# The last product of a two-layer token mixer in seven block products, under a new order of the whole program

## Chip, cores and metric

The program runs on one core of one Trainium2 chip. The metric is the device time of one execution in microseconds (us); the kernel before takes 1402.06 us, the median of three runs (1402.04 to 1402.17). Engines are named as the profile names them: PE (TensorE matmuls), PEld (its weight loads), DVE (VectorE), ACT (ScalarE), POOL (GpSimd), SP (the queue that issues the DMAs).

## The reference, cut

```python
# attention: q, k, v of 8 batches x 8 heads x 576 tokens x 64
out = A @ Z @ C @ v            # softmaxes against 32 landmarks; Z by 6 Newton steps
# first layer, x: 8 x 576 x 512
u  = x + real(fft2(x))
un = normalize(u)
x  = u + relu(un @ w_ch1) @ w_ch2                     # 512 -> 2048 -> 512
# second, gated layer
xk = mu_k * x + (1 - mu_k) * x_prev                   # x_prev: the token before
xr = mu_r * x + (1 - mu_r) * x_prev
k  = relu(xk @ w_k)                                   # 512 -> 1024
v  = k * k @ w_v                                      # 1024 -> 512
out = sigmoid(xr @ w_r) * v
```

## The kernel before

**Stages.** The 4608 tokens are nine blocks of 512 (`NB`, `BLK`). First come the eight batches of the attention (`phase1`, line 730) with the first layer of each block as soon as its tokens are there; batches below `HALF` (line 40) take their Fourier transforms with plain matrices and f32 products, the later ones fold the tokens into halves and use f16 pairs. Then comes the gated stage, one `Gated` object per block (line 1996 on).

**Numbers as pairs.** A value of f32 precision is a pair of f16 tiles, high and low half. A product is the three partial products of `PARTS`. A "split" makes the pair: ACT casts to the high half, DVE or POOL subtracts it for the low half.

**Seven block products.** Both operands are cut in 2 x 2 blocks of 256; sums of blocks are formed and seven products take the place of eight. The first-layer products from block 2 on, the product with `w_k` (`Gated.first`, line 2060) and the gate's with `w_r` (`Gated.gate`, line 2006) are made so. One such product is 12 matmuls of 256 columns. The product of the squared values with `w_v` (`Gated.second`, line 2114, and `last`) is a plain one: per block 8 rows f x 4 token groups j x 3 parts, 96 matmuls of 512 columns into four PSUM banks (`acc`); `store` (line 2143) multiplies each bank by `qi` and the sigmoid `sg` on DVE and issues the output DMA. `first` leaves the squared values as an f16 pair `k2`: per half g and quarter, ACT makes relu and square (`out`, line 2075) and the cast, DVE the low half.

**What sets the order.** Nothing is issued while the program is recorded. `Plan.record` notes every operation with its engine, cost and predecessors, and `Plan.issue` (line 469) simulates the engines with these costs: at each step the engine that is free first takes, of its ready operations, the one with the largest key, the longest way to the end (`tail`) plus a lead, by stage (`NOW` 1000, `SOON` 300, ...) and by part and batch (`LEADS`, line 155). The order so found is written out, one queue per engine. Matmuls marked `chain=True` (line 429) are each a predecessor of the next, so the main products keep the order in which the code records them. `HOP` 0.2 is added between engines; DVE operations that overlap a POOL operation are lengthened (lines 579 to 589). Where PE has a predicted gap, matmuls on zeros (`warm`, line 1423, tile `spare`) are put in.

**The gated stage's order.** `prep(i)` (line 1930) loads a block of the stored first-layer result (`yb`), mixes it with the token before (DVE, ACT) and splits seven sums each for `xk` and `xr`, the low halves on POOL; both operands alternate between two pools. `fillers` (line 2156) lays the steps of `first`, `gate` and the earlier block's `second` between one another.

**Rows of the profile.** Every ACT, DVE and POOL operation is issued in line 267, matmuls in 423, transposes in 440, DMAs in 408.

Of the kernel before, what the change touches and what calls it, by code (L numbers as in the profile page):

```python
# [24 lines left out]
DM = H * D  # L25
# [14 lines left out]
HALF = 2  # L40
# [100 lines left out]
class Op:  # L141
    def __init__(self, index, eng, run, cost, port=0, nbytes=0):
        self.index, self.eng, self.run, self.cost = index, eng, run, cost
        self.port, self.nbytes = port, nbytes
# [3 lines left out]
        self.parted = False  # L148

# [6 lines left out]
    ("back", 0): 808,  # L156
    ("back", 1): 3753,
    ("back", 2): 292,
    ("back", 3): 2,
    ("back", 4): 804,  # L160
    ("back", 5): 255,
    ("back", 6): 170,
    ("back", 7): 349,
    ("keys", 1): -347,
    ("keys", 2): 842,
    ("keys", 3): -200,
    ("keys", 4): -24,
    ("keys", 5): -20,
    ("keys", 6): 10,
    ("keys", 7): 107,  # L170
    ("land", 0): -297,
    ("land", 1): -653,
    ("land", 2): -89,
    ("land", 3): -333,
    ("land", 4): -544,
    ("land", 5): -74,
    ("land", 6): -180,
    ("land", 7): -185,
    ("norm", 0): 138,
    ("norm", 1): 3084,  # L180
    ("norm", 3): -30,
    ("norm", 4): 102,
    ("norm", 6): 511,
    ("norm", 7): -99,
    ("norm", 8): -30,
    ("own", 1): 500,
    ("own", 2): 23,
    ("own", 3): -84,
    ("own", 4): 146,
    ("own", 5): 150,  # L190
    ("own", 6): -6,
    ("own", 7): 404,
    ("pairs", 0): -315,
    ("prep", 1): 70,
    ("prep", 2): 140,
    ("queries", 1): 90,
    ("queries", 2): 148,
    ("queries", 3): 85,
    ("queries", 4): -18,
    ("queries", 5): 301,  # L200
    ("queries", 6): 622,
    ("queries", 7): 11,
    ("series", 1): 1044,
    ("series", 2): -102,
    ("series", 3): -103,
    ("series", 4): -41,
    ("series", 5): -137,
    ("series", 6): -95,
    ("sums", 0): 7,
    ("sums", 1): -85,  # L210
    ("sums", 2): 30,
    ("sums", 3): 448,
    ("w1", 1): -468,
    ("w1", 2): 34,
    ("w1", 3): 376,
    ("w2", 0): 5,
    ("w2", 1): -312,
    ("w2", 3): 246,
# [7 lines left out]
class Engine:  # L226
# [5 lines left out]
    def cost(self, op, outs, ins):  # L232
# [4 lines left out]
        if self.kind == "v":  # L237
            if op in ("tensor_scalar", "tensor_copy") and not psum:
                return (n / 2 + 150) / 960, 2
            if op == "reciprocal":  # L240
                return 0.25, 0
            return (n + 150) / 960, int(read > 1 and op != "tensor_reduce")
        if self.kind == "s":
            scalars = sum(wide(x) == 1 for x in ins) if n > 1 else 0
            more = 0.19 if len(outs) > 1 else 0.0
            more += 0.16 if outs[0].dtype == I8 else 0.05 if ins[0].dtype == I8 else 0.0
            return (0.17 if psum else 0.2) + n * 0.83e-3 + 0.093 * scalars + more, 0
        if op == "memset":
            return 0.1, 0
        return max(0.28, 0.15 + n * 2.28e-3), int(n > 8)  # L250

    def __getattr__(self, op):
        f = getattr(self.eng, op)

        def call(out, *args, **kw):
# [5 lines left out]
            cost, port = self.cost(op, outs, ins)  # L261
# [7 lines left out]
            return self.plan.record(self.kind, run, cost, outs, ins, port)  # L269
# [4 lines left out]
class Plan:  # L274
# [4 lines left out]
    HOP = 0.2  # L279
# [99 lines left out]
    def record(self, eng, run, cost, outs, ins, port=0, nbytes=0):  # L379
        op = self.node(eng, run, cost, port=port, nbytes=nbytes)  # L380
# [34 lines left out]
    def mm(self, out, lhsT, rhs, start, stop, chain=False, beside=1, **kw):  # L415
# [53 lines left out]
    def issue(self):  # L469
# [6 lines left out]
        for op in ops:  # L476
            for p in op.preds:
                p.succs.append(op)
        for op in reversed(ops):
# [12 lines left out]
        shared = both = dma = 0.0  # L492
        warming, parted = [], False

        def ready(op):
# [3 lines left out]
                    p.end + (self.HOP + op.slack if p.eng and p.eng != op.eng else 0.0)  # L499
# [15 lines left out]
        def done(op, end):  # L515
            op.end = end
            for t in holds.pop(op, ()):
                t.left -= 1
                if t.left == 0:
                    bank[t.bank] = max(o.end for o in t.ops) + self.HOP  # L520
# [30 lines left out]
        while any(avail.values()) or any(later.values()) or pending:  # L551
# [27 lines left out]
            free[e] = end = start + op.cost  # L579
            if e == "g" and op.port:  # L580
                shared = end
                if both > t:
                    free["v"] += 0.5 * min(both - t, op.cost)
            elif op.port and shared > t:
                over = shared - t
                end += min(0.5 * over, op.cost) if op.port == 1 else min(0.6 * over, 0.5)
                free[e] = end
            if e == "v" and op.port:
                both = end
# [140 lines left out]
def phase1(a, iss, psum, const, pool, ident, ublock, ones, early):  # L730
# [385 lines left out]
    def chain_c(b):  # L1116
# [56 lines left out]
        for g in range(2):  # L1173
            for c in range(5):
                kk = 128 if c < 4 else 64
                for hh in range(4):
# [5 lines left out]
                        c in (0, 2), c in (1, 4), tile_position=(0, 32 * hh),  # L1182
# [193 lines left out]
def build(nc, tc, a):  # L1376
# [5 lines left out]
    with stack, tc.manual_schedule():  # L1382
# [36 lines left out]
        iss.warm_from = g_.memset(zero, 0.0)  # L1419
        iss.lead = START  # L1420
# [16 lines left out]
        def rows_of(name, r, g):  # L1437
# [4 lines left out]
            "w_v0": [128, 2, 4, DM], "w_v1": [128, 2, 4, DM],  # L1442
# [39 lines left out]
        far_items = [  # L1482
# [820 lines left out]
```

## Time and profile before

| | us |
|---|---|
| median of three runs | 1402.06 |
| span of the profiled execution | 1401.8 |
| PE busy | 1389.2 |
| DVE busy | 1019.0 |
| ACT busy | 807.3 |
| POOL busy | 456.3 |
| matmuls on zeros | 23.6 |

A row of a timeline begins with its start and its length in us. Matmuls follow one another before the earlier one has ended, so the distance of two starts is what a matmul costs, and its length is more. A row of the chain has the start, the time up to the next link, engine, tile, line and count. A row of windows gives a stretch and its length, the busy time of PE, PEld, DVE, ACT and POOL with the count of instructions in brackets, the granted clock of PE, and the share and GB/s of the DMA engines. A row of a group gives the count, the busy time with the mean in ns of one, and the idle time before it.

### The profile page before, as it was taken

The page shows a single profiled execution, that of the slowest core. Times are in us where ns is not written, and L with a number is a line of the kernel's source. Part 1 is how long each engine was busy: PE and PEld are TensorE (multiplying, and loading weights), DVE is VectorE, ACT ScalarE, POOL GpSimd, SP SyncE. Part 2 cuts the span into 40 slices and gives each one's busy share as a digit, 9 for nine tenths or more (in the row PEclk, how much of TensorE's full clock was granted, in tenths as well). Part 3 has the DMA queues.
Part 4 walks back from the last instruction along what each step waited for, and adds up shares of the span by engine and source line. Part 5 has one row for each costly group of instructions (what it writes and reads, how often), then busy time and mean ns, then how long its engine had stood idle before and what let it go on. Part 6 is the DMA issues. An engine that isn't in the chain of part 4 may idle for free.

```text
span 1401.8 us, 26994 instructions
## 1 busy us (share of the span) xinstructions
PE 1389.2 (99%) x10648; PEld 906.1 (65%) x10648; DVE 1019.0 (73%) x2055; ACT 807.3 (58%) x1603; POOL 456.3 (33%) x546
## 2 busy tenths in 40 slices
PE   9999999999999999999999999999999999999998
PEld 5555454576676676676676666666767767776775
DVE  7897985886987876976966566837679788786332
ACT  4876543445545545545553445526787877786552
POOL 3013163532523422423332030603445552444000
PEclk9999999999999999999999999999999999999999
DMA  9795673655554554653556776423011011100001
GB/s 353 272 329 187 229 264 102 211 195 190 190 199 139 197 204 127 248 174 118 172 186 246 240 270 235 157 82 121 31 50 62 12 61 61 61 1 31 31 8 54
DMA packets 87071, 213.71 MB, mean 152 GB/s; under 512 B 7200, under 2 KB 28704, under 8 KB 80672
## 3 DMA queue, kind: packets, MB, share of 16 engines
q1 hardware_dynamic: 86944, 211.98, 43.4%
q8 instruction: 84, 1.38, 0.4%
q14 instruction: 43, 0.35, 0.1%
HBM read 168.71 MB, written 43.25 MB: 151 GB/s over the span
## 4 chain that ended last, share of the span: by engine, by line
PE 97%; DVE 1%; ACT 1%; issue 0%; POOL 0%; DVEq 0%; ACTq 0%; POOLq 0%
PE acc L423 40%; PE ph L423 36%; PE gp L423 18%; PE gp L440 3%; PE spare L1429 1%; DVE xt L267 1%; DVE bdY L267 0%; ACT Y L267 0%; DVE uc L267 0%; DVE ub L267 0%; ACT rm L267 0%; POOL Ae L267 0%; ACT L267 0%; ACT Ae L267 0%; ACT xk L267 0%
## 5 line engine op out<-in xcount | busy, mean ns | idle before, releaser
L423 PEld LDWEIGHTS <-w 128*128 128x128 f16 x4464 | 429.9, 98 | 264.8 <-issue 29.7
L423 PE MATMUL acc<-h,w 128*128 128x512 f16 x1728 | 430.8, 379 | 0.0
L423 PE MATMUL ph<-un,w 128*128 128x256 f16 (+1 forms) x2736 | 393.8, 288 | 1.4 <-DVE un L267 1.4
L423 PE MATMUL acc<-w_v,k 128*128 128x512 f16 x864 | 204.6, 379 | 0.0
L423 PE MATMUL ph<-xk,w_k 128*128 128x256 f16 x1512 | 180.1, 273 | 0.0
L267 DVE TENSOR_TENSOR rm<-ph,rm 128x512 f32<-128x512 f32 x138 | 95.1, 689 | 115.9 <-ACT rm L267 72.0
L267 ACT ACTIVATE rm<-ph 128x512 f32<-128x512 f32 x156 | 92.8, 595 | 139.2 <-PE ph L423 137.9
L423 PEld LDWEIGHTS <-w_k 128*128 128x128 f16 x1512 | 147.9, 98 | 27.9
L423 PEld LDWEIGHTS <-k 128*128 128x128 f16 x864 | 84.5, 98 | 78.2
L267 POOL TENSOR_TENSOR xr<-xt,xr 128x512 f16<-128x512 f32 x63 | 84.2, 1358 | 91.2 <-DVE gm L267 50.6
L267 POOL TENSOR_TENSOR xk<-xt,xk 128x512 f16<-128x512 f32 x63 | 86.9, 1397 | 60.6 <-ACT xk L267 60.1
L423 PE MATMUL gp<-w_r,xr 128*128 128x256 f16 x756 | 93.5, 273 | 1.7 <-ACT sg L267 1.3
L267 ACT ACTIVATE rm<-rm 128x512 f32<-128x512 f32 (+1 forms) x134 | 84.3, 630 | 16.6 <-DVE rm L267 12.4
L423 PEld LDWEIGHTS <-xr 128*128 128x128 f16 x756 | 73.8, 98 | 22.7 <-issue 1.9
L267 ACT ACTIVATE h<-rm 128x512 f16<-128x512 f32 x84 | 52.6, 626 | 50.1 <-DVE rm L267 49.5
L267 DVE SCALAR_TENSOR_TENSOR xt<-yb,mus,xt 128x512 f32<-128x512 f32 x72 | 60.9, 882 | 23.0 <-POOL xt L267 21.7
L267 DVE SCALAR_TENSOR_TENSOR k<-rm,k 128x512 f16<-128x512 f32 x72 | 58.0, 810 | 22.9 <-ACT k L267 22.8
L267 DVE SCALAR_TENSOR_TENSOR h<-rm,h 128x512 f16<-128x512 f32 x84 | 65.0, 778 | 10.5 <-ACT h L267 9.9
L267 DVE TENSOR_TENSOR xt<-xt 128x512 f32<-128x512 f32 x52 | 64.3, 1244 | 6.9 <-POOL xk L267 4.2
L267 ACT ACTIVATE h<-ph 128x512 f16<-128x512 f32 x60 | 35.7, 595 | 42.3 <-PE ph L423 42.2
L267 POOL TENSOR_TENSOR A<-A,sm 100x512 f32<-100x512 f32 (+1 forms) x24 | 26.9, 1122 | 93.4 <-DVE sm L267 79.9
L267 POOL TENSOR_TENSOR sq<-sq 128x512 f32<-128x512 f32 x18 | 23.9, 1327 | 96.1 <-ACT sq L267 96.1
(227 smaller groups left out, 2078.3 us busy)
## 6 DMA issues: line engine op xcount, KB each, us to landing
w<-dw SPq DMA_DIRECT2D x60, 1024.0 KB, 7.3
w<-dwp SPq DMA_DIRECT2D x56, 384.0 KB, 5.7
ys<-ub SPq DMA_DIRECT2D x36, 256.0 KB, 7.4
out<-sg SPq DMA_DIRECT2D x35, 256.0 KB, 2.1
yb<-ys SPq DMA_DIRECT2D x8, 1026.0 KB, 5.3
v<-in_v SPq DMA_DIRECT2D x8, 1024.0 KB, 7.0
wst<-in_w_ch SPq DMA_DIRECT2D x16, 512.0 KB, 5.9
q<-in_q SPq DMA_DIRECT2D x14, 580.0 KB, 8.1
```

The costliest lines, as they stand in the source:

```text
L267: f(real(out), *map(real, args), **{k: real(x) for k, x in kw.items()})
L423: self.nc.tensor.matmul(out.real(), lhsT=lhsT.real(), rhs=rhs.real(), start=start, stop=stop, **kw)
L440: self.nc.tensor.transpose(out.real(), in_.real(), ident.real())
L1429: nc.tensor.matmul(into.real() if into else spare[0], lhsT=z.to_broadcast([128, 128]), rhs=z.to_broadcast([128, 512]), start=not into, sto ...
```

## The change

**Product with w_v.** `k2` is now f32 and only a staging tile (`stage`), squared in one step with the scale inside. `forms` makes the seven sums of token and feature blocks and splits them, 1024 columns at a time (four differences on DVE, seven casts on ACT, seven low halves on DVE). `second(w, x)` is one of the seven products, 24 matmuls of 256 columns in two steps; its result is copied out of PSUM (ACT), summed (DVE) and written out per half of the columns. `w_v` is converted in four pairs of rows, as `w_k` is, and stored as seven block sums. `xr` is now one tile that all later blocks share; the order of the stage is written as strings of steps.

**Batch 1** is folded (`HALF` 1).

**The plan.** A cost now has a latency and a shorter time of occupation (`hold`); the costs, `HOP` by engine, and the exclusion of DVE and POOL are new; `LEADS` are new; the order of the main products is no longer a predecessor but only lengthens the `tail`. ACT runs one exponential on zeros at the start. The products of v go over chunks first, then over the two groups.

```diff
-HALF = 2
+HALF = 1
...
-    ("norm", 0): 138,
+    ("norm", 0): 27116,
...
-    HOP = 0.2
+    HOP = {"v": 0.035, "s": 0.035, "g": 0.08, "pe": 0.055, "sp": 0.1, None: 0.035}
+    DRAIN = 0.2
...
         if chain:
             op.lead = 0.0
             if self.chained:
-                op.preds.add(self.chained)
+                op.after = self.chained
...
-            op.tail = cost + max([
-                s.tail + (self.HOP if s.eng != op.eng and op.eng else 0.0) for s in op.succs
-            ] or [0.0])
+            op.tail = cost + max(
+                [s.tail + self.hop(op, s) for s in op.succs] + [tails.get(op, 0.0)]
+            )
+            if op.after:
+                tails[op.after] = op.tail
...
-            free[e] = end = start + op.cost
-            if e == "g" and op.port:
-                shared = end
...
+            if op.port:
+                if locked != e and lock > start:
+                    start = max(start, lock - 0.06)
+                locked, lock = e, start + op.cost
+            end = start + op.cost
+            free[e] = start + op.hold
...
-        for g in range(2):
-            for c in range(5):
+        for c, g in [(c, g) for c in range(4) for g in range(2)] + [(4, 0), (4, 1)]:
...
+        s_.activation(iss.tile(com, [128, 2], F16, "table"), zero, AF.Exp)
...
-            "w_v0": [128, 2, 4, DM], "w_v1": [128, 2, 4, DM],
+            "w_v": [128, 2, 7, 4, HB],
...
+        far_pairs += [
+            ([rows_of("w_v", r, 0) for r in (f, f + 4)], kept["w_v"][:, :, :, f]) for f in range(4)
         ]
...
+            xk = [iss.tile(pb2 if i % 2 else pb, [128, 7, 2, HB], F16, "xk", "xk" + x) for x in "hl"]
+            xr = iss.tile(pool, [128, 2, 7, 2, HB], F16, "xr")
...
-                    s_.activation(t, t, AF.Square)
...
-                    s_.activation(hi, t, AF.Copy, scale=scale)
-                    v_.scalar_tensor_tensor(lo, t, scale, hi, op0=ALU.mult, op1=ALU.subtract)
+                    s_.activation(
+                        k2[:, z, 2 * a:2 * a + 2], t.rearrange("p (f n) -> p f n", f=2), AF.Square,
+                        scale=1.0 / (8 * WS),
+                    )
...
+            def split(self, at, t):
+
+                hi, lo = self.form[at]
+                s_.activation(hi, t, AF.Copy)
+                v_.tensor_tensor(lo, t, hi, op=ALU.subtract)
+
+            def forms(self, g):
...
+                if g == 0:
+                    self.place("ub_0", 0, 4)
+                    self.split(0, b11)
+                    v_.tensor_tensor(b11, b12, b11, op=ALU.subtract)
+                    self.split(4, b11)
+                    return
...
+                v_.tensor_tensor(b11, b22, b11, op=ALU.subtract)
+                self.split(5, b11)
+                v_.tensor_tensor(b12, b22, b12, op=ALU.subtract)
+                self.split(6, b12)
+                v_.tensor_tensor(b11, b21, b11, op=ALU.subtract)
+                self.split(3, b11)
+                self.split(2, b22)
+                self.split(1, b21)
...
+            def second(self, w, x, order=(0, 1)):
...
+                    for f in range(4):
+                        for n, (y, z) in enumerate(PARTS):
+                            mm(
+                                ps[:, HB * j:HB * j + HB],
+                                self.form[x][y][:, f, 128 * j:128 * j + 128], wv[w][:, z, f],
...
+                if w == 0:
+                    copy(ps, t=t1)
+                elif w == 4:
+                    copy(ps, t=t2)
+                elif w == 5:
+                    copy(ps, t=t3)
+                    v_.tensor_tensor(t3, self.steps["b"], t3, op=ALU.add)
+                    self.out(t3, 1, 1)
...
+            order = "fgfgfgsfsgfsgfsfgsgs" if before else "fgfgfgfgfgff"
...
+            for x in "ffsfssfsftftftt" if before else "fftfttftfff":
+                next(kinds[x])
...
+        for x in ((1, 1), (4, 5), (5, 6), (6, 2), (2, 3)):
+            for _ in block.second(*x):
+                pass
```

In the strings f is a step of `first` (12 matmuls of 256 columns), g one of `gate`, s one of the earlier block's `second`, t one of the own block's.

## Rows read from the trace of the kernel before

**Rows 1.** The page: span, engine totals, and engines of the chain that ended last.
```profile
span 1401.8 us, 26994 instructions
...
PE 1389.2 (99%) x10648; PEld 906.1 (65%) x10648; DVE 1019.0 (73%) x2055; ACT 807.3 (58%) x1603; POOL 456.3 (33%) x546
...
PE 97%; DVE 1%; ACT 1%; issue 0%; POOL 0%; DVEq 0%; ACTq 0%; POOLq 0%
```

**Rows 2.** Windows: head, batches with first layer, gated stage.
```profile
0.00:70.00 70.00, 65.24 (x500) 38.97 (x501) 57.09 (x151) 46.25 (x111) 13.50 (x28) 0.95 0.88 313
70.00:957.00 887.00, 885.10 (x6971) 557.71 (x6970) 660.64 (x1516) 451.72 (x950) 281.74 (x351) 1.00 0.57 196
957.00:1397.50 440.50, 438.82 (x3180) 309.38 (x3178) 300.41 (x388) 309.33 (x545) 161.07 (x167) 1.00 0.12 41
```

**Rows 3.** Windows: a gated block with, and one without, operands to make.
```profile
1219.00:1267.00 48.00, 48.00 (x352) 33.98 (x350) 39.06 (x45) 36.12 (x63) 19.70 (x14) 1.00 0.06 23
...
1315.00:1364.00 49.00, 49.00 (x356) 34.55 (x354) 14.46 (x22) 23.76 (x41) 0.00 (x0) 1.00 0.06 22
```

**Rows 4.** The chain that ended last, in the gated stage; a weight-load group by form.
```profile
1137.51 2.62 PE ph L423 x24
1142.74 2.59 PE acc L423 x12
...
1162.52 1.31 PE gp L423 x12
...
1191.19 2.59 PE acc L423 x12
...
L423 PEld LDWEIGHTS <-xr 128*128 128x128 f16 x756 | 73.8, 98 | 22.7 <-issue 1.9
```

**Rows 5.** Timeline of DVE, and one row of POOL's, in a gated block.
```profile
1163.00 0.67 DVE L267 TENSOR_TENSOR xt<-xt,gp 128x512 f32<-128x512 f32 x1
...
1164.20 1.27 DVE L267 TENSOR_TENSOR xt<-xt,gp 128x512 f32<-128x512 f32 x2
...
1174.97 6.25 DVE L267 TENSOR_TENSOR xt<-xt 128x512 f32<-128x512 f32 x4
...
1173.70 6.96 POOL L267 TENSOR_TENSOR xr<-xt,xr 128x512 f16<-128x512 f32 x5 [15.28 <-DVE gm L267]
```

**Rows 6.** End: timeline from the last product on.
```profile
1384.39 13.11 PE L423 MATMUL acc<-w_v,k 128*128 128x512 f16 x60
...
1385.32 1.29 ACT L267 ACTIVATE rm<-rm 128x512 f32<-128x512 f32 x2 [0.65 <-DVE rm L267]
...
1394.95 0.75 DVE L267 SCALAR_TENSOR_TENSOR sg<-acc,qi,sg 128x512 f32<-128x512 f32 x1 [1.84 <-PE acc L423]
...
1397.55 0.88 DVE L267 SCALAR_TENSOR_TENSOR sg<-acc,qi,sg 128x256 f32<-128x256 f32 x2 [1.84 <-PE acc L423]
```

**Rows 7.** The chain in batch 1 (three rows), then batch 2: transforms, mixed, unmixed.
```profile
118.25 2.24 PE gp L423 x18
...
125.29 1.95 PE gp L423 x8
...
132.00 0.69 PE gp L423 x4
...
195.33 0.90 PE gp L423 x13
...
223.17 1.49 PE gp L423 x12
...
230.95 0.47 PE gp L423 x6
```

**Rows 8.** Head: the group of matmuls on zeros, and rows of two timelines.
```profile
L1429 PE MATMUL spare<-zero 128*128 128x512 f16 x80 | 23.6, 432 | 1.9 <-POOL zero L267 1.9
...
12.66 1.28 ACT L267 ACT_TABLE_LOAD   x1 [12.66 <-DVE cst L267]
...
20.31 1.38 PE L423 MATMUL gp<-v,ET 128*32 128x64 f32 x52
```

More of the change, by code (lines that the diff above doesn't have):

```diff
@@ L141, with __init__ @@
 class Op:
-    def __init__(self, index, eng, run, cost, port=0, nbytes=0):
+    def __init__(self, index, eng, run, cost, port=0, nbytes=0, hold=None):
         self.index, self.eng, self.run, self.cost = index, eng, run, cost
+        self.hold = cost if hold is None else hold
         self.port, self.nbytes = port, nbytes
@@ L200 @@
[L200 to L218, printed above, removed]
+    ("back", 1): 338,
+    ("back", 2): 3860,
+    ("back", 3): 319,
@@ new lines @@
+    ("back", 4): 264,
+    ("back", 6): -101,
+    ("back", 7): 1251,
+    ("keys", 1): 8413,
+    ("keys", 3): 315,
+    ("keys", 4): -98,
+    ("keys", 5): 2816,
+    ("keys", 6): 1797,
+    ("keys", 7): 847,
+    ("land", 0): -453,
+    ("land", 1): 90,
+    ("land", 2): -4569,
+    ("land", 3): -931,
+    ("land", 4): 230,
+    ("land", 6): 832,
+    ("land", 7): -6866,
+    ("norm", 0): 27116,
+    ("norm", 1): 968,
+    ("norm", 2): 2159,
+    ("norm", 3): 53,
+    ("norm", 5): 4475,
+    ("norm", 6): 71,
@@ new lines @@
+    ("norm", 7): 624,
+    ("norm", 8): 561,
+    ("own", 0): 1915,
+    ("own", 2): 331,
+    ("own", 3): 44,
+    ("own", 4): 100,
+    ("own", 5): 393,
+    ("own", 6): 151,
+    ("own", 7): -102,
+    ("pairs", 0): -2266,
+    ("prep", 0): -101,
+    ("prep", 1): 348,
+    ("prep", 2): -188,
+    ("prep", 3): 231,
+    ("prep", 4): 9,
+    ("prep", 5): -36,
+    ("prep", 6): -197,
+    ("prep", 7): -1,
+    ("prep", 8): 3,
+    ("queries", 1): -129,
+    ("queries", 2): 70,
+    ("queries", 3): -74,
@@ L267, in run, with hop @@
                 f(real(out), *map(real, args), **{k: real(x) for k, x in kw.items()})
-            return self.plan.record(self.kind, run, cost, outs, ins, port)
+            return self.plan.record(self.kind, run, cost, outs, ins, port, hold=hold)
         return call
 class Plan:
-    HOP = 0.2
+    HOP = {"v": 0.035, "s": 0.035, "g": 0.08, "pe": 0.055, "sp": 0.1, None: 0.035}
+    DRAIN = 0.2
+    def hop(self, p, op):
+        if not p.eng or p.eng == op.eng == "pe":
+            return 0.0
+        return self.HOP[op.eng] + (self.DRAIN if p.eng == "pe" else 0.0)
     def __init__(self, nc, shadow):
@@ L519, in done @@
                 if t.left == 0:
-                    bank[t.bank] = max(o.end for o in t.ops) + self.HOP
+                    bank[t.bank] = max(o.end for o in t.ops) + self.HOP["pe"]
             for s in op.succs:
@@ L1863, in background @@
                 weights.pair(*x)
-            iss.part = "items", 0
-            for x in far_items:
-                weights.run(*x)
             iss.part = None
@@ L2131, in last @@
-            def last(self, j):
-                iss.lead = NOW
-                sl = slice(128 * j, 128 * j + 128)
-                for f in self.order[4:]:
-                    for n, (x, y) in enumerate(PARTS):
-                        mm(
-                            self.acc[j], self.ks[f // 4][:, x, f % 4, sl],
-                            ws[f"w_v{f // 4}"][:, y, f % 4], False,
-                            f == self.order[-1] and n == 2, chain=True,
-                        )
-                self.store((j,), 2 if j == 3 else 1)
@@ new lines, in chain @@
+        def chain(*steps):
+            for x in steps:
+                yield from x
+        blocks = {}
+        rooms3 = None
+        held = iter(())
+        for i in range(NB):
+            blocks[i] = block = Gated(i)
+            if i == 0:
+                stage[0] = iss.spot(pb, [128, 2, 4, HB], F32, "s0", "yb_0")
+            gate = block.gate()
+            before = blocks.get(i - 1)
+            late = iter(())
+            if before:
+                late = chain(before.second(4, 5), before.second(5, 6), before.second(2, 3))
+            kinds = dict(f=block.first(0), g=gate, s=late)
+            order = "fgfgfgsfsgfsgfsfgsgs" if before else "fgfgfgfgfgff"
+            for x in order:
+                next(kinds[x])
+            if i == 0:
+                next(gate), next(gate)
+                t = iss.spot(pb, [128, 3584], F32, "s1", "xr_0")
+                stage[1] = t[:, 0:2048].rearrange("p (z f n) -> p z f n", z=2, f=4)
+                rooms3 = [t[:, 2048 + 512 * n:2560 + 512 * n] for n in range(3)]
+            own = chain(block.second(0, 0), block.second(3, 4))
+            late = chain(before.second(6, 2), before.second(1, 1)) if before else own
+            kinds = dict(f=block.first(1), s=late, t=own)
+            for x in "ffsfssfsftftftt" if before else "fftfttftfff":
+                next(kinds[x])
+            if not before:
+                continue
```

295 lines of the change are left out of this document (135 added, 160 removed).

## The prediction

> **What bounds the kernel now.** I read the engine totals and the chain first. TensorE is busy 99% of the span and carries 97% of the chain that ended last [rows 1]. That share is an average, so next come three stretches [rows 2]. In 70 to 957 us (batches 1 to 7 and the first layer) TensorE idles 1.9 us of 887; in 957 to 1397.5 us (the gated stage) 1.7 us of 440.5. Only the head and the last 4.3 us, after it, hold time in which it does nothing useful: in the head 4.8 us idle and, besides, matmuls on zeros that the planner puts into predicted gaps (part 4). So a term of the sum is worth what it takes off TensorE's list, as long as VectorE (DVE) and ScalarE (ACT) keep up. The second thing to see is how near they are: in a gated block with the next block's operands being made, DVE is busy 39.1 of 48 us and ACT 36.1; in one with none to make, 14.5 and 23.8 of 49 [rows 3].
>
> **Part 1, seven block products.** Removed per block: 96 matmuls of 512 columns. Added: 7 products of 24 matmuls of 256 columns, 168. Twelve of the first kind follow one another in 2.59 us, twenty-four of the second in 2.62 [rows 4]; the gate's products, which like the new ones have an activation as the stationary side and a weight as the moving one, take the same 1.31 per twelve. So 8 x 2.59 = 20.7 against 7 x 2.62 = 18.3 us: 2.4 per block, 21.4 us over nine blocks. All of it lies on TensorE, in a stretch that idles 1.7 us.
>
> The weight load of a matmul takes 98 ns by the trace [rows 4], under the 109 ns spacing, so it stays covered. One rule speaks against this part. The Trainium skill, page "TensorE: Matmul & The Clock Gate", section "Back-to-back issue gap", gives sustained spacings of about 131 ns per matmul at 512 columns and 81 ns at 128; an estimate from it for 256 is 98 ns, by which the block would go from 12.6 to 16.4 us and the kernel would lose 35 us. The trace disagrees with it: 216 and 109 ns.
>
> **Part 2, what the products cost beside TensorE.** DVE in a block without operands to make is 14.5 us. It loses 8 low-half operations (0.68 each, as in [rows 5]) and 4 output multiplications (0.75 [rows 6]): 6.0 stay. It gains three sums from PSUM (2.1), eight half-width output multiplications (two take 0.88 [rows 6], so 3.5), and four differences and seven low halves of 1024 columns. No 1024-column DVE operation stands in the trace; two of 512 columns back to back take 1.27 [rows 5], one takes 0.68, so each is between 0.68 and 1.27; 1.25 is taken, since a second 512 columns has never been free. 11 x 1.25 = 13.8. Together 25.4. Making the next block's operands costs 39.1 - 14.5 = 24.6 more, of which much is waiting for GpSimd (POOL): four DVE differences take 6.25 us beside five POOL operations of 6.96 us, 1.56 each where one alone takes 0.68 [rows 5]. So DVE needs 25.4 + 24.6 = 50.0 us per block if operations stand alone; where they stand in a queue each starts 0.60 after the one before instead of 0.68, and 55 operations at 0.08 give 4.4 back: 45.6. The TensorE block is 48.4 us (the same product stands at 1142.74 and at 1191.19 in the chain [rows 4]); the new one is 2.4 less, 46.0. DVE therefore goes from four fifths full to about full. For ACT I count, against 36.1: minus 8 casts, plus 7 casts of 1024 columns and 3 copies, some 4 us more, 40 of 46; not the bound.
>
> What follows for TensorE is bounded so. Below: nothing, if the queue is dense and the eight blocks that have a next one are helped by the first block, which has no second product of an earlier one, and the last, which makes no operands. Above: 8 x (50.0 - 46.0) = 32 us, if no operation overlaps and waits for POOL stay as they are. I take 7, nearest the dense end, because DVE in the rows does run at 0.60 when it has a queue; it is not nothing, because POOL's 14 operations per block [rows 3] now meet the differences and low halves too, which read two SBUF operands as the differences of [rows 5] do. On this the Trainium skill, page "SBUF — State Buffer", section "Who interferes with whom", says that a DVE operation with two SBUF inputs and a POOL operation that reads SBUF shut each other out for the whole instruction. The trace agrees: 1.56 us per DVE operation beside POOL, 0.68 without.
>
> The gate's operand xr becomes single, so the next xr may be written only after the gate's seventh product, near the end of a block's first 20 steps; behind it wait ACT's casts and POOL's low halves. Seven POOL operations of 1.39 are 9.7 us, the second half has 15 steps of 1.31, 19.7 us: covered; without that cover the next gate would wait. Outputs go out in eight DMAs of half the size per block instead of four, and w_v comes in seven pieces, 3.7 MB instead of 2.1: SP issues them well ahead and the DMA engines are 12% busy in the stage [rows 2]. Nothing is charged.
>
> **Part 3, batch 1 folded.** 36 transform matmuls in 4.5 us (eighteen in 2.24) become 48 in 3.1 (twelve in some 0.77; the row has one more of another kind); 8 f32 products in 3.9 us (1.95 per eight records, two of a product) become 24 in 3.0 (1.49 per twelve); the unmixed sums go from 4 x 0.69 to 4 x 0.47 [rows 7]. 1.4 + 0.9 + 0.9 less 0.1 for one more small product: 3.1 us off TensorE, where it idles 1.9 of 887. The added DVE work (about 5 us of low halves and folds) and the larger conversion of w_v (four pairs instead of eight single rows, some 6 us of DVE, 4 of ACT, 14 of POOL) lie in the same stretch, DVE 660.6, POOL 281.7 of 887 [rows 2]; at no cover they would cost those few us, not more.
>
> **Part 4, the head.** ACT loads its table for 1.28 us at 12.66 while the first exponentials wait [rows 8]; loading it ahead takes that out of batch 0's chain. The products of v now end with 16 of 80 matmuls after the last transposed block, not half; 52 of them took 1.38 us [rows 8]: up to 0.9. Both are in front of a chain in which 23.6 us are zeros [rows 8], and the norm of block 0 is put ahead of all else. But the whole order is new on all engines. Bounds: a gain of up to 8 (what a third of the zeros is worth), a loss of 5 (the idle time of the head, once more). I take a gain of 2, the two steps that have rows.
>
> **Part 5, the end.** Before, sixty matmuls run to the end without a gap, and 4.3 us follow (last operations at 1397.55 [rows 6], span 1401.8 [rows 1]). After, the last five products need their operands first: from the last first-layer product on, sum 0.69, relu and square 1.29 [rows 6], difference 1.25, cast about 1.05 (between the 0.63 of 512 columns and twice that [rows 6]), low half 1.25, about 5.5 with 2.6 us of second product as cover; then a copy (0.6) must be made before the same bank goes on, twice. 1 to 5 us; I take 3, less 0.4 for one last multiplication instead of two: 2.6.
>
> **Order as a preference** can fill the 1.9 and 1.7 us of idle time [rows 2] and no more; counted at nothing, inside the bounds.
>
> **Sum.** 1401.8 - 21.4 - 3.1 - 2 + 7 + 2.6 = 1384.9. The median of the runs is 1402.06, 0.26 over the profiled span: 1385.
>
> **Rivals.** (a) DVE becomes the bound of the gated stage. For: 50.0 us per block when counted singly. Against: in the rows a full queue runs at 0.60. It decides from 46.0 us of DVE per block, and from 46.0 + (24.5 + 2 - 2.6)/8 = 49.0 the kernel is slower. At 50.0 the time is 1385 - 7 + 32 = 1410. Between 47.8 and 48.8 it is 1392 to 1400. (b) The new plan hides all of it and the head gains 6: 1385 - 7 + 1 - 4 = 1375. For it: DVE at 45.6 just fits, and the two end blocks leave some 30 us spare. (c) The matmuls of 256 columns cost more than half of the 512s. It decides from 20.7/168 = 123 ns; if load and matmul stood in a row, 98 + 109 = 207 ns, 14.1 us per block more, 1385 + 21 + 127 = 1533. The gate's rows nearly exclude it. By the spacing that the Trainium skill states ("TensorE: Matmul & The Clock Gate", "Back-to-back issue gap") the time would be 1385 + 21 + 35 = 1441, an estimate of the same kind. (d) The change doesn't do what it says: the new plan's order loses elsewhere what TensorE saves, 1402.
>
> **How the numbers follow.** Forecast (1379 to 1392) 0.52; (b) 1370 to 1379, 0.22; (a) mild 0.14, (a) slower 0.07; (c) 0.01; (d) 0.04. 0.2% of 1402 is 2.8 us, about what a measurement can tell from no change. Faster 0.52 + 0.22 + 0.14 = 0.88; same 0.04; slower 0.08. The range 1373 to 1400 leaves out about a third of (b) and the slower and equal cases.
>
> **What would show it.** Right: 1512 matmuls of 256 columns in place of the 864, spaced 109 ns; a block period of 46 to 47 us; DVE over 90% busy up to the last block; a wait of 1 to 3 us in front of the last five products; 48 transform matmuls in batch 1. Wrong: PE waits for DVE in each gated block (rival a); a period over 48; a head that ends after 70 us.

## The result, and the profile after

The changed kernel takes 1389.14 us, the median of four runs (1387.0 to 1390.19), against 1402.05 for the kernel before: a ratio of 0.9906, 95% interval 0.9893 to 0.9919. The forecast was 1385 us, in a range of 1373 to 1400. The profiled execution has a span of 1388.4 us, 13.4 less than before.

The page after: span, engine totals, engines of the chain that ended last; then groups (count, busy us with the mean ns of one, idle time before them).

```profile
span 1388.4 us, 28583 instructions
...
PE 1368.6 (99%) x11297; PEld 966.2 (70%) x11297; DVE 1102.0 (79%) x2182; ACT 830.3 (60%) x1633; POOL 491.2 (35%) x572
...
PE 88%; DVE 4%; ACT 3%; DMA 2%; POOL 1%; issue 1%; SPq 0%; ACTq 0%; DVEq 0%; POOLq 0%
...
L451 PE MATMUL acc<-w_v,k 128*128 128x256 f16 x1512 | 183.3, 273 | 3.1 <-DVE k L289 1.8
...
L451 PEld LDWEIGHTS <-k 128*128 128x128 f16 x1512 | 147.7, 98 | 21.2 <-DVE k L289 2.4
...
L289 POOL TENSOR_TENSOR xr<-xt,xr 128x512 f16<-128x512 f32 x63 | 98.7, 1585 | 50.3 <-ACT xr L289 50.1
...
L289 DVE TENSOR_TENSOR k<-s,k 128x1024 f16<-128x1024 f32 x63 | 84.5, 1362 | 9.3 <-ACT k L289 9.3
```

TensorE (PE) is at 99% as in [rows 1], busy for 20.6 us less; DVE is busy for 83 us more, POOL for 35. In the chain PE fell from 97% to 88%. Next the windows after, to be read beside [rows 2, 3]: head, batches with first layer, gated stage, then one gated block, then 300 us of the gated stage.

```profile
0.00:70.00 70.00, 65.44 (x595) 42.06 (x596) 54.78 (x183) 42.80 (x110) 16.38 (x31) 0.85 0.82 283
70.00:957.00 887.00, 879.70 (x6853) 549.54 (x6852) 663.77 (x1519) 454.47 (x955) 300.29 (x369) 1.00 0.57 198
957.00:1385.20 428.20, 423.49 (x3853) 374.63 (x3850) 382.95 (x481) 333.00 (x568) 174.52 (x172) 1.00 0.14 49
...
1103.87:1149.95 46.08, 46.08 (x427) 41.31 (x425) 44.76 (x56) 37.88 (x65) 21.42 (x22) 1.00 0.14 47
...
1000.00:1300.00 300.00, 299.61 (x2759) 268.48 (x2757) 290.64 (x360) 246.64 (x425) 135.44 (x130) 1.00 0.13 43
```

Three things are new. In a block DVE is busy 44.8 of 46.1 us, 97% over 300 us, where it was 39.1 of 48 [rows 3]; PE still runs without a gap. The granted clock of the head is 0.85, not 0.95. And PE idles 7.3 us of 887, not 1.9. The chain, for the costs and the period (start, time to the next link):

```profile
73.11 3.18 PE ph L451 x14
...
102.65 0.77 PE gp L451 x12
...
122.09 1.49 PE gp L451 x12
...
1103.87 1.53 PE gp L451 x16
...
1117.20 1.31 PE acc L451 x12
...
1123.75 2.62 PE acc L451 x24
...
1149.95 1.53 PE gp L451 x16
...
1196.02 1.53 PE gp L451 x16
```

Twenty-four new matmuls take 2.62 us, as charged from [rows 4]; the same place of the block returns after 46.08 and 46.07 us, before after 48.45. Batch 1 has transforms of twelve in 0.77 and products of twelve in 1.49, where [rows 7] show eighteen in 2.24 and eight in 1.95. The first long run of first-layer matmuls starts at 73.11 us; before, it started at 68.47.

The time by stage, cut at the start of that run and at the first and last matmul of the gated stage:

| stage | before | after | difference |
|---|---|---|---|
| head, to the first layer | 68.47 | 73.11 | +4.6 |
| first layer to gated stage | 890.9 | 891.5 | +0.6 |
| gated stage, first to last matmul | 438.1 | 420.5 | -17.6 |
| after the last matmul | 4.3 | 3.2 | -1.0 |

The end, PE's timeline (in brackets the idle time before a row and what ended it):

```profile
1365.73 2.78 PE L451 MATMUL acc<-w_v,k 128*128 128x256 f16 x24
1369.70 2.79 PE L451 MATMUL acc<-w_v,k 128*128 128x256 f16 x24 [1.19 <-DVE k L289]
1373.11 5.19 PE L451 MATMUL acc<-w_v,k 128*128 128x256 f16 x46 [0.61 <-DVE k L289]
1378.99 4.09 PE L451 MATMUL acc<-w_v,k 128*128 128x256 f16 x36 [0.69 <-ACT s L289]
1383.71 1.47 PE L451 MATMUL acc<-w_v,k 128*128 128x256 f16 x12 [0.62 <-DVE sg L289]
```

Four waits, 3.1 us, in a stretch that ran without a gap before [rows 6]. Last, DVE beside POOL in a gated block, two rows of POOL's timeline and two of DVE's:

```profile
1109.80 1.16 POOL L289 TENSOR_TENSOR xk<-xt,xk 128x512 f16<-128x512 f32 x1 [8.02 <-ACT xk L289]
...
1118.32 7.32 POOL L289 TENSOR_TENSOR xr<-xt,xr 128x512 f16<-128x512 f32 x4 [0.91 <-ACT xr L289]
...
1122.44 2.17 DVE L289 TENSOR_TENSOR k<-s,k 128x1024 f16<-128x1024 f32 x1
...
1142.92 1.22 DVE L289 TENSOR_TENSOR k<-s,k 128x1024 f16<-128x1024 f32 x1
```

A low half of 1024 columns takes 1.22 us, and 2.17 while POOL reads beside it; POOL's four take 1.83 each there, where one takes 1.16 while DVE's operations beside it read PSUM (at 1109.80 us). The 1.39 of [rows 5] already stood beside DVE's differences. That is the exclusion which the Trainium skill, page "SBUF — State Buffer", section "Who interferes with whom", describes; the trace agrees, on both engines.

### The profile page after: what moved, and what is told of

Read it like the earlier page. It is cut to its first block, busy times and chain, and to the rows that moved or that the text cites. A ratio compares the mean times of both kernels' runs of the same rounds, so it can differ in the third digit from the quotient of the medians.

```text
span 1388.4 us, 28583 instructions
## 1 busy us (share of the span) xinstructions
PE 1368.6 (99%) x11297; PEld 966.2 (70%) x11297; DVE 1102.0 (79%) x2182; ACT 830.3 (60%) x1633; POOL 491.2 (35%) x572
## 3 DMA queue, kind: packets, MB, share of 16 engines
q1 hardware_dynamic: 98848, 215.13, 44.8%
## 4 chain that ended last, share of the span: by engine, by line
PE 88%; DVE 4%; ACT 3%; DMA 2%; POOL 1%; issue 1%; SPq 0%; ACTq 0%; DVEq 0%; POOLq 0%
PE acc L451 35%; PE ph L451 34%; PE gp L451 17%; PE gp L468 2%; DMA dw_v<-wboth 1%; DMA v<-in_v 1%; DVE uc L289 1%; DMA k<-in_k 1%; DMA wst<-in_w_ch 0%; DVE RX L289 0%; DVE ks L289 0%; SPq L436 0%; DVE s L289 0%; DVE k L289 0%; DVE cst L289 0%
## 5 line engine op out<-in xcount | busy, mean ns | idle before, releaser
L451 PE MATMUL acc<-w_v,k 128*128 128x256 f16 x1512 | 183.3, 273 | 3.1 <-DVE k L289 1.8
L451 PE MATMUL ph<-xk,w_k 128*128 128x256 f16 x1512 | 184.8, 273 | 0.4 <-ACT rm L289 0.4
L451 PEld LDWEIGHTS <-k 128*128 128x128 f16 x1512 | 147.7, 98 | 21.2 <-DVE k L289 2.4
L289 POOL TENSOR_TENSOR xr<-xt,xr 128x512 f16<-128x512 f32 x63 | 98.7, 1585 | 50.3 <-ACT xr L289 50.1
L289 DVE TENSOR_TENSOR k<-s,k 128x1024 f16<-128x1024 f32 x63 | 84.5, 1362 | 9.3 <-ACT k L289 9.3
L289 DVE SCALAR_TENSOR_TENSOR h<-rm,h 128x512 f16<-128x512 f32 x84 | 61.2, 731 | 13.3 <-ACT h L289 12.7
L289 ACT ACTIVATE k<-s 128x1024 f16<-128x1024 f32 x63 | 65.3, 1050 | 5.2 <-DVE s L289 5.2
L289 DVE SCALAR_TENSOR_TENSOR xt<-yb,mus,xt 128x512 f32<-128x512 f32 x72 | 57.4, 832 | 6.2 <-POOL xt L289 6.2
L289 DVE SCALAR_TENSOR_TENSOR h<-ph,h 128x512 f16<-128x512 f32 x60 | 41.2, 687 | 23.8 <-ACT h L289 23.4
L289 POOL MEMSET xt<- 128x1 f32 x64 | 5.9, 98 | 133.8 <-ACT xt L289 75.7
```

The source lines that it names most:

```text
L289: f(real(out), *map(real, args), **{k: real(x) for k, x in kw.items()})
L451: self.nc.tensor.matmul(out.real(), lhsT=lhsT.real(), rhs=rhs.real(), start=start, stop=stop, **kw)
```

## The experiments

Theory: DVE is the second bound and just fits under the new PE block, so the gain is PE's and no more can be had there. Rivals: DVE has slack that its busy share hides; the order of the plan, not the products, brings the gain; the head's clock or the end's cover holds back a further gain.

The gated stage's length in the profiled executions, and the medians, in one table (changed kernel first). Starts are those of its first matmul, ends those of its last. A start holds what the clock did in the head of that one execution (section "Head and end").

| kernel | median us | ratio to before (95%) | gated stage starts | lasts |
|---|---|---|---|---|
| changed | 1389.1 | 0.9893 to 0.9919 | 964.6 | 420.5 |
| one more DVE operation | 1395.6 | 0.9940 to 0.9970 | 967.3 | 428.8 |
| two more, same order | 1408.4 | 1.0027 to 1.0057 | 961.7 | 441.5 |
| two more, planned anew | 1409.6 | 1.0036 to 1.0078 | 962.9 | 442.1 |
| two of three parts, same order | 1382.2 | 0.9840 to 0.9869 | 961.3 | 414.9 |
| two of three parts, planned anew | 1398.3 | 0.9947 to 0.9976 | 961.4 | 431.4 |
| batch 1 plain | 1403.2 | 0.9997 to 1.0022 | 975.3 | 420.6 |
| strict order | 1440.7 | 1.0263 to 1.0294 | 981.8 | 453.5 |
| new products, plan of before | 1461.5 | 1.0413 to 1.0447 | 979.3 | 476.7 |
| old products, new plan, old leads | 1421.9 | 1.0111 to 1.0147 | 979.0 | 438.6 |
| old products, new plan and leads | 1421.9 | 1.0109 to 1.0159 | 977.3 | 437.4 |
| more zeros | 1388.5 | 0.9890 to 0.9920 | 962.2 | 420.6 |
| more zeros, other end | 1387.5 | 0.9879 to 0.9911 | 963.8 | 418.1 |

### Is DVE full?

One more operation per block, then two, with every other instruction in the changed kernel's order (in `split`, the operation is issued twice); and the two under a plan that knows of them.

```diff
-                self.split(5, b11)
+                self.twice(self.split(5, b11))
...
-                self.split(6, b12)
+                self.twice(self.split(6, b12))
```

> The changed kernel with one more VectorE (DVE) operation of 1024 columns per gated block (the low half of sum 5 is subtracted twice in a row), planned as if it were not there, so that the order on every engine stays that of the changed kernel. Each is 1.14 to 1.21 us. Theory A (about 1.1 us of slack per block): 0 to 3 us, 1389 to 1392. Theory B (no slack at all; two more under a new order cost 21 us in the gated stage): 9 x 1.2 = 11 us, 1400. Theory C (a new order, not the work, cost those 21 us): 0 to 1 us here.

> The same with two more per block (low halves of sums 5 and 6), order kept as in the changed kernel. Theory A (slack of about 1.1 us per block): 9 x (2.4 - 1.1) = 12 us, 1401. Theory B (no slack): 9 x 2.4 = 21 us, 1411. Theory C (the new order made the 21 us of the replanned run): 0 to 4 us, 1389 to 1393.

```diff
                 self.split(5, b11)
+                v_.tensor_tensor(self.form[5][1], b11, self.form[5][0], op=ALU.subtract)
...
                 self.split(6, b12)
+                v_.tensor_tensor(self.form[6][1], b12, self.form[6][0], op=ALU.subtract)
```

> The changed kernel with two more VectorE (DVE) operations of 1024 columns in each gated block that makes operands (the low halves of two sums are subtracted twice; the second writes the same values). Alone such an operation takes 1.14 to 1.21 us by the changed kernel's trace, so DVE gets 2.3 to 2.4 us more per block, 8 blocks or so, 19 us in all. Theory A (DVE is about full: it needs some 45 of the 46.05 us of a block, as the dense count of the prediction gave 45.6): about 1.1 us of slack per block are used up and the rest shows, 8 x 1.3 = 10 us, between 8 and 18, 1397 to 1407 us, with a wait of TensorE (PE) for DVE in each block. Theory B (DVE has slack that its busy share hides, because its operations stretch when it has time): 0 to 3 us, 1387 to 1392, no such wait.

Nine blocks run `forms(1)`, so the first adds 9 operations; in a queue they start 1.14 us apart, so 10.3 us of DVE. Of these 6.4 us show in the medians and 8.2 in the gated stage of the profiled execution, which is the slowest of seven and runs at half the granted clock from 1380.5 to 1383.9 us. The second operation adds as much again and shows 12.8 more in the medians. The engines of the chain with two more, then the same place of the block in the chain with one more:

```profile
PE 70%; DVE 20%; ACT 4%; DMA 3%; issue 1%; POOL 1%; SPq 0%; DVEq 0%; ACTq 0%; POOLq 0%
```

```profile
1119.10 0.68 DVE rm L289
...
1166.09 0.68 DVE rm L289
```

The chain now runs through DVE for a fifth of the span, not 4%. A block takes 47.0 us with one more operation and 48.3 with two, where the changed kernel has 46.07: 1.14 us of work cost 0.9, and 2.28 cost 2.2. By these periods the slack is 0.1 to 0.2 us per block, less than the 1.1 of theory A. One more, 1395.6 us, lies between theory A (up to 1392) and theory B (1400); two more, 1408.4, are nearest to theory B (1411). A new plan for the two changes nothing (442.1 against 441.5), so theory C falls; its median, 1409.6, is above the 1407 that theory A of that run allowed.

DVE's busy time is not all its own work: the low half of 2.17 us above holds about 1 us in which POOL shut it out. No run took work off POOL, so how much of the full DVE is POOL's is not shown. PE's waits in the gated stage of the kernel with two more, longest sums first (us in total, times, longest):

```profile
PE gp L451 <- DVE gm L289: 4.4, 5, 1.2
PE acc L451 <- DVE k L289: 4.3, 2, 2.4
PE gp L451 <- ACT sg L289: 3.8, 5, 1.2
PE ph L451 <- ACT rm L289: 3.5, 3, 2.1
```

### What would less work on PE bring?

Two of three partial products with `w_v`: 6.1 us of PE per block less. First planned anew, then with the plan of the changed kernel.

```diff
-                        for n, (y, z) in enumerate(PARTS):
+                        for n, (y, z) in enumerate(PARTS[:2]):
```

> The changed kernel with two of the three partial products in each of the seven block products with w_v: 112 matmuls of 256 columns per block instead of 168. The part of the result that the third partial product carries is left out. TensorE (PE) gets 56 x 0.1092 = 6.1 us per block less to do, 55 us over nine blocks; nothing changes on the other engines. Theory A (DVE stands right behind PE as the next bound, some 45 of 46 us per block): the block falls only to what DVE needs, about 45 us, so the eight blocks with operands to make gain about 1 us each and the last block its 6.1: 10 to 20 us, 1369 to 1379, and PE waits for DVE several us in every block. Theory B (PE alone bounds the stage and DVE has slack): nearly all of it, 1389 - 55 = 1334, at most 1345.

```diff
         def run():
+            if skip:
+                return
             self.nc.tensor.matmul(
...
-                                opens and j == 0 and f == 0 and n == 0, f == 3 and n == 2,
-                                chain=True, skip_group_check=True,
+                                opens and j == 0 and f == 0 and n == 0, f == 3 and n == 1,
+                                chain=True, skip_group_check=True, skip=n == 2,
```

> The changed kernel with two of the three partial products in each product with w_v (what the third carries is left out), planned as if all three were there: the order of everything else is that of the changed kernel, and TensorE (PE) has 56 x 0.109 = 6.1 us per block less, 55 us in all. The run with the same cut under a new plan was 9 us slower than the changed kernel, 1398. Theory A (DVE's work, some 45 us per block, bounds the stage as soon as PE's falls below): eight blocks fall by about 1 us, the last by 6: 1374 to 1381. Theory B (the new plan's order was at fault, PE is the one bound): under 1345. Theory C (the loop over DVE, ScalarE and GpSimd with its waits is longer than DVE's own work, about 48 us per block as in the replanned run): 1385 to 1400, though PE has less to do.

With the order kept, 55 us off PE shorten the gated stage by 5.7 us and the kernel by 7. The engines of the chain of that kernel, a window of 300 us of the gated stage, and PE's longest waits there:

```profile
PE 62%; DVE 24%; ACT 8%; issue 2%; DMA 2%; POOL 1%; SPq 0%; DVEq 0%; ACTq 0%; POOLq 0%
```

```profile
1000.00:1300.00 300.00, 271.75 (x2405) 236.71 (x2404) 292.96 (x361) 244.51 (x424) 133.50 (x130) 0.98 0.13 43
```

```profile
PE ph L453 <- ACT rm L289: 11.0, 9, 3.8
PE gp L453 <- ACT gm L289: 9.5, 7, 2.3
PE gp L453 <- DVE gm L289: 8.4, 8, 1.7
```

PE falls from 299.6 to 271.8 busy us of 300, DVE goes from 97 to 98%, and the blocks of 46.07 us take 45.1 to 46.6. So the stage is bound by DVE and the waits around it as soon as PE's block is shorter than 46 us: theory A (1374 to 1381) is missed by a microsecond, B (under 1345) falls, and what C puts down to waits shows in the three rows. The replanned kernel lost 16 us against it; its theories, which both forecast under 1380, missed, because they took a new plan to be as good as the old one. DVE waits 12.8 us for POOL's `xt` in its gated stage, 5.5 with the order kept.

### Plan, products, batch 1

Each of the parts alone. Batch 1 as before:

```diff
-HALF = 1
+HALF = 2
```

> The changed kernel with HALF = 2, so that batch 1 is not folded, all else the same. Theory A (the fold takes 3.1 us off TensorE in a stretch that TensorE bounds): 3 us more than the changed kernel, 1392. Theory B (what the fold adds on VectorE in the head and up to 200 us, sixteen short sums of 3.45 us among it, gives it back): no difference or up to 2 us less, 1387 to 1389.

The gated stage lasts as long, 420.6 us, but starts 10.7 us later than in the profile of the changed kernel, and 13.6 to 14.0 later than in two profiles with that kernel's order and full clock from 25 to 40 us (below); the medians differ by 14.0. Both theories (1392, and 1387 to 1389) missed. 3.1 us are PE's work as counted; PE idles 12.2 us of 70 to 955, where the changed kernel idles 7.3 and the kernel before 1.9. So undoing 3.1 us of work costs 14 us of time. What is left over is put down to the order, whose leads were not fitted to this list of work; it was not tried with leads of its own.

The main products' order made a predecessor again:

```diff
                 op.after = self.chained
+                op.preds.add(self.chained)
```

> The changed kernel with each main product again a predecessor of the next. Theory A (the order as a preference can fill only single microseconds of TensorE's idle time): 0 to 3 us over the changed kernel, 1389 to 1392. Theory B (with VectorE 98% busy in the gated stage the free order is what keeps TensorE from waiting): TensorE waits in each gated block, 1396 to 1410.

Its largest group of PE's waits in the gated stage, and the same of the kernel with the new products under the plan of before (old class of costs, old hop, old leads, strict order):

```profile
PE gp L451 <- ACT gm L289: 19.4, 8, 6.1
```

> The changed kernel's products and folded batch 1 under the plan of before: its costs, hops, its lengthening of overlapped VectorE operations, strict order of the main products, and its leads. Theory A (the seven products need the new plan, since VectorE is nearly full): TensorE waits for VectorE in the gated blocks by 1 to 3 us each, 1395 to 1410, while the head is as long as before, first layer at 69 us. Theory B (the products bring the gain by themselves): 1383 to 1388, below the changed kernel by the head's 4 us.

```profile
PE gp L423 <- ACT gm L267: 29.5, 9, 7.4
```

Both show the same thing: the gate's next product stands at PE's front while ACT's copy of the gate's bank is late, and what stands behind it may not pass. With the order free that wait is gone; the changed kernel has 1.6 us of waits in the gated stage before the last five products. Both lost more than any theory had (up to 1410): 33 and 56 us in the gated stage, 17 and 15 ahead of it. Both were planned anew with leads that were fitted to something else, so the loss is not shown to be the strict order's alone.

Then the other way about, the old products and plain batch 1 under the new plan, with old and with new leads. Edit: the classes of operation, engine and plan of the changed kernel put into the kernel before, without or with its `LEADS`.

> The kernel before (its eight products, batch 1 plain) under the changed kernel's plan: occupation and latency apart, the new prices, the recorded order of the main products as a preference; the leads of the kernel before. Theory A (the plan has little to give to the old work, since PE idled 1.9 and 1.7 us in its two long stretches, and costs where its leads are not fitted): 1400 to 1410 us. Theory B (the plan is itself worth a good part of the gain): under 1398. Either way the gated stage should keep its 438 us, since PE idles 1.7 us in it; a difference can only come from before it.

> The kernel before (eight products, batch 1 plain) under the changed kernel's plan with the changed kernel's leads. With the leads of before this plan gave 1421.9 us, 20 us late at the start of the gated stage. Theory A (the leads are fitted to one list of work and one plan; new leads on the old work are no better fitted): 1410 to 1430. Theory B (plan and leads carry a gain of their own that the old work can use): under 1400.

Both are 20 us slower than before, with the gated stage at its old 438 us; all of the loss lies ahead of it. Theory B falls in both; theory A holds with the new leads (1410 to 1430) and was too low with the old ones (to 1410). So, with the leads at hand, neither the products nor the plan gains alone (1461.5 and 1421.9 against 1402); together they do. The leads were not fitted anew for any of these kernels, so the figures do not say what each part could give at its best; that was not tried.

### Head and end

More zeros in the head's predicted gaps:

```diff
-                ] * int((idle - 0.15) / 0.3)
+                ] * (int((idle + 0.3) / 0.3) if idle > 0.3 else 0)
```

> The changed kernel with one number changed: in a predicted gap of TensorE over 0.3 us the planner puts one or two more matmuls on zeros; the order of all else is the same. Theory A (the head is longer than before because fewer zeros, 47 instead of 80, let the granted clock fall to 0.50 in 25 to 40 us): the clock stays near 1.0 there, the first matmul of the first layer starts at 69 to 70 us instead of 73.1, and the time is 3 to 4 us under the changed kernel's, some 1385.5. Theory B (the head is longer because the new order serves it worse): the clock is better but the start of the first layer moves by less than 1 us, 1388 to 1390.

The group of zeros, then the windows of 20 to 40 us, changed kernel:

```profile
L1456 PE MATMUL spare<-zero 128*128 128x512 f16 x47 | 16.7, 487 | 1.9 <-POOL zero L289 1.9
```

```profile
20.00:25.00 5.00, 3.25 (x23) 1.45 (x12) 4.55 (x17) 2.36 (x6) 0.91 (x2) 0.81 1.02 405
25.00:40.00 15.00, 14.58 (x59) 10.27 (x60) 9.58 (x24) 8.33 (x21) 5.08 (x8) 0.50 0.98 352
```

The same two with more zeros:

```profile
L1456 PE MATMUL spare<-zero 128*128 128x512 f16 x72 | 20.5, 421 | 1.9 <-POOL zero L289 1.9
```

```profile
25.00:40.00 15.00, 13.66 (x91) 8.64 (x89) 11.61 (x30) 11.49 (x29) 7.72 (x10) 1.00 0.98 349
```

In these two executions the granted clock is at half (1.2 GHz) from 25 to 40 us with 47 zeros and full (2.4 GHz) with 72, and the gated stage starts 2.4 us earlier. That does not show that the zeros did it. The two kernels above with the order kept (two more DVE operations, two of three parts) have the 47 zeros and run the changed kernel's instructions, in its order, up to 990 us. The same window in the second of them:

```profile
25.00:40.00 15.00, 11.65 (x82) 7.84 (x82) 11.91 (x33) 10.84 (x27) 7.75 (x9) 1.00 1.06 367
```

There the clock is full with 47 zeros, in the other kernel too, and the gated stage starts at 961.7 and 961.3 us, earlier than with 72; in the kernel with one more operation, again the same up to there, the clock is at 0.51 in this window. So the same head loses the clock in some executions and not in others: in the changed kernel's own four runs the granted clock goes from 0.993 to 0.999 and the span from 1388.4 to 1385.2. Whether more zeros make the loss rarer is not shown; the median gains 0.6 us, inside both intervals, and lies in theory B's range while the clock is theory A's. Without the loss the first layer starts at 70.10 us, not 73.11. So 3.0 of the head's 4.6 us are the clock of the profiled execution; the other 1.6 stay with full clock in that window and are the new order's (in which step was not tried).

The end: the same zeros, the last store not held back, and in the last block two first-layer products earlier so that own second products are left as cover.

```diff
-                late = self.i == NB - 1 and w == 2
+                late = False
...
-            for x in "ffsfssfsftftftt" if before else "fftfttftfff":
+            for x in ("ffsfssfsfftfttt" if i == NB - 1 else "ffsfssfsftftftt") if before else "fftfttftfff":
```

> The changed kernel with three edits: more zeros in the head's predicted gaps (as in the run with more zeros alone, 1388.5 us), in the last block the sums of the first half taken in another order of the recorded steps, so that two first-layer products stand earlier and own second products are kept as cover for the last sums, and the last store not held back. Theory A (the four waits of PE near the end, 3.1 us together, are for lack of cover): 1 to 2 us go, 1386.5 to 1387.5 us. Theory B (the waits follow the chain sum, relu, difference, cast, low half, which no cover shortens): the same 1388 to 1389 us, with the waits at other places. Either is a difference that only several rounds can tell.

```profile
1363.41 6.93 PE L451 MATMUL acc<-w_v,k 128*128 128x256 f16 x62
1370.59 5.20 PE L451 MATMUL acc<-w_v,k 128*128 128x256 f16 x46 [0.26 <-DVE k L289]
1376.47 5.40 PE L451 MATMUL acc<-w_v,k 128*128 128x256 f16 x48 [0.69 <-ACT s L289]
```

Two of the four waits are gone and one is down to 0.26: 3.1 us become 0.95, and the gated stage lasts 418.1 instead of 420.5 us. The last store, no longer held back, gives 0.5 of this back after the last matmul (3.8 us, not 3.2). Theory A holds in the trace. In the medians it is 1387.5 against 1389.1 and 1388.5, with intervals that overlap; it is the lowest median of a kernel that does all the work, and whether it is faster than the changed kernel by these runs stays open.

## Why the prediction was right, and where it was not

Right in sign and within its range, 4 us from the value. By its own terms, in the profiled executions:

| term | forecast | measured |
|---|---|---|
| seven products | -21.4 | -21.3 (nine times 48.45 less 46.08) |
| waits of PE for DVE in the gated stage | +7 | 0 (1.6 us idle before the last five products; 1.7 before) |
| end | +3 - 0.4 | +3.1 - 1.0 |
| batch 1 folded | -3.1 | +0.6 for the whole stretch |
| head | -2 | +4.6, of which 3.0 the clock |
| sum | -16.9 | -14.0, and +0.6 that no row accounts for |

**Products.** 1512 matmuls at 109 ns, weight load 98 ns and covered. Rival (c) fell at once: the spacing that the Trainium skill gives ("TensorE: Matmul & The Clock Gate", "Back-to-back issue gap"), by the prediction's estimate from it, would have lengthened the block, and the trace shows it shortened by the 2.4 us that [rows 4] gave.

**Waits for DVE.** The mechanism was right and the size off. The dense count, 45.6 us per block, was nearer than the 50.0 of single operations: the block shown has 44.8. The 7 us were a choice between the ends that the dense end did not need. The experiments show how near it was: rival (a) was to decide from 46.0 us, and 1.14 us more per block already cost 0.9 of it. That POOL was slowed (1585 ns for `xr`, 1358 before) shows in no wait of PE. Of what was counted at nothing here, the shared `xr`, the eight output DMAs and the larger `w_v`, no wait of PE in the stage names a DMA, and one of 1.2 us stands at the gate.

**End.** Forecast 3 us of waits, measured 3.1, most of it from the chain that was named: difference, cast, low half, then the copy before the same bank goes on. The last wait, 0.62, is for an output multiplication (`sg`), which the chain did not have.

**Head.** This step failed, as its own sign (a head that ends after 70 us) said it would show. The two removed costs are there: the table is loaded at 0.73 us and no longer before the exponentials, and the products of v come in one run. Still the first layer starts 1.6 us later than before where the clock is full from 25 to 40 us, so the rest of the new order lost more than the two steps gave; where is open. The other 3.0 us are half clock in that window of the profiled execution, for which the prediction had no term. It counted the zeros, now 47 instead of 80 [rows 8], only as time to win; whether they also help to keep the clock up is open. The bounds (8 won, 5 lost) held the +4.6; the value taken from them had the wrong sign.

**Batch 1.** The 3.1 us of work are gone from PE's list, but PE idles 5.4 us more up to 955 us; the largest waits that the kernel before does not have are for DVE's `RX` (2.1) and `un` (1.1) and POOL's `s` (0.7). "Where it idles 1.9 of 887" was a property of the order before, not of the stage: a fitted order was replaced, and its fit went with it (the reading that the runs with one part changed support, though none of them had leads of its own).

**Order as a preference, counted at nothing.** The order's worth was read off the idle time of the kernel before, whose list of work suited a strict order. For the new list it is not nothing: strict again, and planned anew without other leads, the time is 1440.7. It belonged into the sum as the condition under which the 7 us can be 0. The two large misses (+7 too much in the gated stage, 10 too little ahead of it, 3 of these the clock) have opposite signs; that the sum came so near is luck. Rival (d), an order that loses elsewhere what PE saves, came true in part: the gated stage starts 5.2 us later in the profile, about 2 later where the clock is kept (961.3 and 961.7 against 959.4).

## What to carry to other kernels

An engine that is 99% busy pays out what is taken off its list only down to the next engine's need per block: count that one densely (starts 0.60 us apart in a queue, not 0.68 each) and see how far the block may shrink, here to 45 or 46 us. A fitted order is part of the work it was fitted to: change the list or the planner alone and the time grows, here by 14 to 60 us. And look at the granted clock of the same stretch in several executions before a difference of a few us in one profile is put down to an edit: here one and the same order of the first 990 us ran with and without a loss of 3 us.

## What the runs showed of the hardware

One wait can cost twice. In the kernel with two of three parts PE waits 3.81 us and runs on at half the granted clock: twelve matmuls take 2.72 us until they end and the next eight 1.92, where twelve take 1.47. Windows and timeline of PE in that kernel:

```profile
1040.00:1045.00 5.00, 1.86 (x18) 1.51 (x16) 3.53 (x3) 4.16 (x6) 2.44 (x4) 0.94 0.00 0
1045.00:1050.00 5.00, 4.34 (x21) 3.09 (x21) 4.47 (x5) 4.08 (x7) 0.10 (x1) 0.50 0.00 0
```

```profile
1036.02 1.47 PE L453 MATMUL ph<-xk,w_k 128*128 128x256 f16 x12
...
1045.66 2.72 PE L453 MATMUL ph<-xk,w_k 128*128 128x256 f16 x12 [3.81 <-ACT rm L289]
1048.17 1.92 PE L453 MATMUL acc<-w_v,k 128*128 128x256 f16 x8
```

Waits of 0.6 to 1.2 us near the end of the changed kernel left the granted clock at 1.00 from 1365 to 1385 us; in the kernel with two of three parts waits of 1.25 and 0.94 us, up to 1093.2 and 1094.6 us, stand right before a stretch at 0.50 from 1095.6 us. So the kernels with long waits show somewhat more loss than their waits alone.
